# Attention on TensorE by two pairs of heads in one visit, all by quarters of the array

**Chip, cores, metric.** One core of one Trainium2 chip. The metric is the device time of one execution in microseconds (us). Each kernel was executed several times, in turns with the kernel before on the same chip. All times quoted are medians with the lowest and highest in brackets.

## The reference

Attention with RMS-normalised queries and keys (8 batches, 12 heads, 448 positions, head size 64), then a two-layer network with Silu on the 3584 x 768 result. All is float32.

```python
def _attn_ref(q, k, v, g_q, g_k):                     # (8, 12, 448, 64) each
    q_n, k_n = rmsnorm(q, g_q), rmsnorm(k, g_k)       # x / sqrt(mean(x*x) + 1e-6) * g
    scores = np.matmul(q_n, k_n.transpose(0, 1, 3, 2)) / np.sqrt(64)
    attn = np.exp(scores - max)
    attn = attn / (sum of attn + 1e-09)
    return np.matmul(attn, v)
# bridge: (B,H,S,D) -> x (B*S = 3584, H*D = 768)
def _moe_ref(x, w_in, w_out):                         # w_in (768, 2048), w_out (2048, 768)
    h = x @ w_in
    return (h * (1.0 / (1.0 + np.exp(-h)))) @ w_out
```

## The kernel before

The two big products use seven half-size products in place of eight (the class `Seven` and the sums of weights and of `x`). They run on TensorE group by group, a group being two batches. Attention of the next group is dealt in between the products: `fill` runs a share of the products of the group before. Attention goes by pairs of heads, since two heads of 64 fill the 128 rows of the array. Scores take 64 rows and 128 columns at a time, two heads beside each other. Weighted sums take 128 rows and 64 columns. The last 64 keys of two pairs share a 128-row unit and already run by quarters (64 x 64).

```python
def transpose(n, name):                      # n: a pair of heads
    t = ps.tile([P, BANK], F32, name=tr(max(n - 1, 0)))      # one PSUM bank, one tile
    ...
    else:
        for j in range(columns // P):
            nc.tensor.transpose(t[:, ts(j, P)], state[n]["k"][:, ts(j, P)], ident)
        if n < 2 * z.NPAIR:                                   # first group: ScalarE
            nc.scalar.activation(kT[:, 0:columns], t[:, 0:columns], AF.Copy, scale=gains)
        else:                                                 # later: VectorE, once per pair
            nc.vector.tensor_scalar_mul(out=kT[:, 0:columns], in0=t[:, 0:columns], scalar1=gains)

def scores(n, *units):
    for j in units:
        banks = ps.tile([P, 2, BANK], F32, name="sc", bufs=2)
        ...                                                   # two heads: 64 x 128 each
        nc.scalar.activation(e[j][:, h, :], banks[:, h, 0:S], AF.Exp, scale=...)

def weigh(n, *units): ...                                     # 128 x 64, accumulates over keys
def unload(n): nc.scalar.copy(xT(*pairs[n]), state[n]["av"])  # divided later, in SBUF

for n in range(last + 2):                                     # 48 visits, one pair each
    ... scores(n, 0, 1) ... weigh(n - 1, LEFT - 1) ... add_up ... unload(n - 1)
    transpose(n + 1, "q"); weights_in(n, 0); fill(); weights_in(n, 1)
    divide_by_sums(n); scores(n, LEFT - 1) ...
    transpose(n + 1, "k") ... weights_in(n, 2); fill(); weights_in(n, 3); normalise(n + 3)
```

`weights_in` rounds pieces of `w_in`: ScalarE opens one ("L90" in the profiles of the changed kernel below), VectorE takes three steps ("L113" to "L120"), GpSimd one ("L124"). It also forms sums of the rounded weights.

## Time and profile before

| | before |
|---|---|
| time | 1446.68 us (1445.59 to 1447.4, 3 runs) |
| TensorE busy | 97% of 1446.8 us |
| streaming passes, summed over the timeline | 1326 us |
| lost between them | 121 us |
| of which idle before a matmul (over 60 ns) | 34.2 us |
| of which half clock (20.8 us of it, so half is lost) | 10.4 us |
| changes of the array's form (the rows and columns that a matmul takes) | 365 |

All rows but the first two are worked out from the trace. "Streaming" is the sum of full passes at the spacing seen in undisturbed runs of matmuls (0.376 us for 448 columns). "Lost" is the rest of the span. Idle time comes from the matmul records, and half clock from the records of the granted clock.

The view of TensorE's waits says what the 34.2 us were spent on. The columns are the tile and line that waited, the releaser, the total in us, the number of times, and the longest.

```profile
PE mm L624 <- DVE parts L575: 5.6, 7, 1.4
PE end L470 <- DVE work L546: 4.7, 5, 2.3
PE mm L542 <- DVE work L523: 4.7, 2, 3.5
PE end L465 <- ACT x L528: 3.5, 2, 2.2
```

No single wait costs much.

### The profile page before, as it was taken

To read this page: it belongs to the slowest core of one execution; us is meant where nothing else is said; L and a number is where in the kernel's file an instruction comes from. 1 tells how busy PE (TensorE), PEld (TensorE's weight loads), DVE (VectorE), ACT (ScalarE), POOL (GpSimd) and SP (SyncE) were. 2 spreads that over 40 slices of the span, in tenths; PEclk is the share of its full clock that TensorE was granted. 3 is DMA by queue.
4 is the path that set the end of the run, shared out by engine and by line. 5 is a ranking of instruction groups with operands and counts; after the bars stand their busy time and mean duration, and the time that the engine had idled before them with its cause. 6 is when DMAs were issued, how large, how long until landed. Compare 5 with 4: busy or idle time off the path is not lost.

```text
span 1446.8 us, 14152 instructions
## 1 busy us (share of the span) xinstructions
PE 1407.0 (97%) x5033; PEld 682.5 (47%) x5033; DVE 710.1 (49%) x941; ACT 510.5 (35%) x859; POOL 388.2 (27%) x255
## 2 busy tenths in 40 slices
PE   8898999999999999999999999999999999999998
PEld 4333443433444444444444445555555555555554
DVE  5888877766645545654544787721222222222220
ACT  6775456644454455445454354300000000000000
POOL 5564444532323333333421144400000000000000
PEclk9999999999999999999999999999999999999999
DMA  6634245422232232223221267332222222222210
GB/s 184 173 100 115 68 145 146 123 69 72 65 99 73 62 111 62 70 79 94 67 84 42 80 190 227 118 114 74 89 80 82 79 80 81 78 84 80 84 59 25
DMA packets 133269, 137.69 MB, mean 95 GB/s; under 512 B 58052, under 2 KB 113860, under 8 KB 133188
## 3 DMA queue, kind: packets, MB, share of 16 engines
q1 hardware_dynamic: 133120, 136.63, 31.7%
q8 instruction: 42, 0.69, 0.2%
q14 instruction: 39, 0.32, 0.1%
q10 hardware_dynamic: 68, 0.05, 0.0%
HBM read 88.47 MB, written 41.29 MB: 90 GB/s over the span
## 4 chain that ended last, share of the span: by engine, by line
PE 83%; DVE 5%; issue 1%; ACT 1%; DMA 0%; POOL 0%; SPq 0%; DVEq 0%; ACTq 0%; POOLq 0%
PE mm L624 38%; PE end L624 14%; PE sc L624 14%; PE sc L486 7%; PE end L512 7%; DVE work L523 1%; PE end L542 1%; PE end L465 1%; DVE work L546 1%; PE end L470 1%; DVE work L474 0%; DVE W L575 0%; DVE parts L575 0%; DVE stage L575 0%; DVE sums_x L572 0%
## 5 line engine op out<-in xcount | busy, mean ns | idle before, releaser
L624 PE MATMUL mm<-x,W 128*128 128x448 f32 x648 | 261.0, 542 | 4.9 <-DVE parts L575 2.0
L494 ACT ACTIVATE work<-sc,rms 128x448 f32<-128x448 f32 x336 | 187.0, 634 | 148.1 <-PE sc L486 92.7
L365 POOL TENSOR_TENSOR rms<-rms,minus_half 128x14 f32<-128x14 f32 (+3 forms) x49 | 168.3, 3435 | 246.7 <-DVE rms L361 231.5
L624 PE MATMUL mm<-sums_x,W 128*128 128x448 f32 x480 | 196.5, 547 | 5.6 <-DVE parts L575 3.6
L624 PEld LDWEIGHTS mm<-x,W 128*128 128x128 f32 x648 | 118.4, 190 | 111.8 <-issue 96.1
L486 PE MATMUL sc<-work 64*128 64x448 f32 (+1 forms) x768 | 160.9, 582 | 2.1 <-ACT work L472 1.3
L523 DVE TENSOR_TENSOR work<-work 128x896 f32<-128x896 f32 x144 | 160.9, 1118 | 1.7
L512 PE MATMUL end<-work,rows 128*64 128x448 f32 (+1 forms) x768 | 152.2, 561 | 0.0
L644 POOL TENSOR_TENSOR parts<-parts,stage 128x448 f32<-128x448 f32 (+1 forms) x37 | 42.1, 1138 | 341.0 <-DVE parts L575 325.1
L624 PEld LDWEIGHTS mm<-sums_x,W 128*128 128x128 f32 x480 | 87.9, 191 | 87.1 <-issue 70.4
L486 PEld LDWEIGHTS sc<-work 64*128 64x128 f32 (+1 forms) x768 | 53.7, 176 | 102.4 <-issue 84.2
L546 DVE RECIPROCAL work<-end 128x448 f32<-128x448 f32 x25 | 73.9, 2956 | 37.3 <-PE end L542 37.2
L644 POOL TENSOR_TENSOR parts<-parts,W 128x384 f32<-128x384 f32 x9 | 8.9, 992 | 307.6 <-DVE parts L575 307.6
L512 PEld LDWEIGHTS end<-work,rows 128*64 128x64 f32 (+1 forms) x768 | 38.3, 135 | 101.5 <-issue 90.7
L575 DVE TENSOR_TENSOR stage<-mm,parts 128x448 f32<-128x448 f32 (+1 forms) x59 | 36.3, 615 | 87.6 <-PE mm L624 49.4
L755 ACT ACTIVATE stage<-stage 128x896 f32<-128x896 f32 x64 | 58.4, 945 | 41.3 <-DVE stage L575 40.3
L631 ACT COPY stage<-mm 128x448 f32<-128x448 f32 (+1 forms) x34 | 17.9, 526 | 152.5 <-PE mm L624 136.4
L624 PE MATMUL mm<-W,work 128*128 128x384 f32 x204 | 68.6, 486 | 0.0
L624 PE MATMUL sc<-W,work 128*128 128x384 f32 x192 | 64.5, 486 | 0.0
L624 PE MATMUL end<-W,work 128*128 128x384 f32 x192 | 64.5, 486 | 0.0
L474 DVE TENSOR_SCALAR work<-end,gains 128x512 f32<-128x512 f32 (+1 forms) x36 | 24.6, 685 | 63.8 <-PE end L470 63.7
L347 DVE TENSOR_REDUCE rms<-qn 112x8 f32<-112x512 f32 x48 | 32.7, 681 | 41.7 <-ACT qn L346 41.7
(135 smaller groups left out, 1772.5 us busy)
## 6 DMA issues: line engine op xcount, KB each, us to landing
hidden<-stage SPq DMA_DIRECT2D x64, 448.0 KB, 2.8
work<-hidden SPq DMA_DIRECT2D x7, 2048.0 KB, 9.7
x<-hidden SPq DMA_DIRECT2D x7, 2048.0 KB, 9.1
W<-in_moe_w_in_dram SPq DMA_DIRECT2D x24, 512.0 KB, 4.4
rows<-in_moe_w_out_dram SPq DMA_DIRECT2D x32, 384.0 KB, 3.3
rows<-in_q_dram SPq DMA_DIRECT2D x48, 224.0 KB, 3.4
rows<-in_k_dram SPq DMA_DIRECT2D x48, 192.0 KB, 3.8
rows<-in_v_dram SPq DMA_DIRECT2D x48, 192.0 KB, 2.7
```

The lines of the kernel that those rows point to most:

```text
L347: nc.vector.tensor_reduce(out=rms[0 : z.R, 0:nq].rearrange("p (h j) -> p h j", h=2), in_=by_head, axis=AX.X, op=ALU.add,)
L365: nc.gpsimd.tensor_tensor(out=flat, in0=flat, in1=half, op=ALU.pow)
L474: nc.vector.tensor_scalar_mul(out=kT[:, 0:columns], in0=t[:, 0:columns], scalar1=gains)
L486: nc.tensor.matmul(banks[ds(i * size, size), h, 0:S], kT[rows, ds(j * P + i * size, size)], qT[m % 2][rows, :], start=True, stop=True,)
L494: nc.scalar.activation(e[j][:, h, :], banks[:, h, 0:S], AF.Exp, scale=rms[n % 4][:, column : column + 1],)
L512: nc.tensor.matmul(state[m]["av"][ds(h * D, D), :], v, e[j][rows, h, :], start=(j == (LEFT if m % 2 else 0)), stop=(j == (LEFT - 1 if m % ...
L523: nc.vector.tensor_tensor(out=t[rows], in0=e[0] if j == 1 else t[rows], in1=e[j][rows], op=ALU.add)
L546: nc.vector.reciprocal(out=r[0], in_=t)
L575: nc.vector.tensor_tensor(out=out, in0=a, in1=b, op=ALU.add)
L624: nc.tensor.matmul(t, self.left(name, s), self.right(name, s), start=s == ends[0], stop=s == ends[1])
L644: nc.gpsimd.tensor_tensor(out=u2, in0=u2, in1=p5, op=ALU.add)
L755: nc.scalar.activation(t, t, AF.Silu)
```

## The change

The intent is to process two pairs of heads (four heads) in one visit. All attention matmuls then take the same form, 64 x 64 quarters with four at once, and the array changes form only at the ends of a visit. The accumulators are divided straight from PSUM. VectorE's small work is dealt out among the products (`fill(others)`). Row sums of the first group are formed by TensorE in three terms.

```diff
+def transpose_k(c):                           # c: two pairs of heads, 24 visits
+    t = ps.tile([P, 2, BANK], F32, name="sc", bufs=2)        # one tile of two PSUM banks
+    rows = place[f"k{c % 2}"]
+    for i in range(2):                                        # i: which pair, its own bank
+        for j in range(z.KEYS + 1 - i):
+            nc.tensor.transpose(t[:, i, ts(j, P)], rows[:, ds((z.KA, z.KB)[i] + j * P, P)], ident)
+        columns = (z.KEYS + 1 - i) * P
+        nc.vector.tensor_scalar_mul(
+            out=kT[:, ds((z.KA, z.KB)[i], columns)], in0=t[:, i, 0:columns], scalar1=gains
+        )
+def scores(c, j, i=None):
+    ...
+            nc.tensor.matmul(
+                banks[ds(half * D, D), h, 0:S], keys[rows, ts(half, D)], qT[rows, pair, :], ...)
+def weigh(c, j, step=0):
+    if step != weighed["step"]:
+        nc.tensor.drain()                     # before the two pairs swap halves of the rows
+        weighed["step"] = step
+    ...
+def divide(c, source):                        # from PSUM, or in place for the first group
+    for i in range(2):
+        nc.vector.tensor_tensor(out=x, in0=x if source is None else source[i], in1=r[i], op=ALU.mult)
-def fill():
-    while filler["due"] > 0:
-        filler["due"] -= next(filler["work"], filler["due"])
+def fill(others=()):
+    ... # runs the products and calls others[dealt]() evenly among them
-    rounds = {(1, 1), (1, 3), (3, 1), ... }   # pieces of w_in at four points of a visit
+    pieces_at = {0: 1, 1: 1, 2: 1, 3: 1, 4: 2, 5: 1, 6: 2, 7: 3}
+    sums_at = {-1: 1, 1: 0, 5: 2, 8: 3}
+def between(c):
+    transpose_q(c + 1)
+    if 0 < c <= EARLY: divide(c - 1, None)
+    ...
+    late = add(c, LEFT - 1) + add(c, LEFT) if c >= GROUP else []
+    further = normalise(c + 2) if c >= GROUP else []
+    fill(late + weights_in(c, 0) + further[2:])
+    transpose_k(c + 1)
+    sum_up(c)
+    ...
+    fill(weights_in(c, 1) + further[:2])
 (cut: loads, normalisation, the order within a visit, start and end)
```

## The prediction

> **What bounds the kernel now.** I read the page first: busy shares, then the chain that ended last, by engine.
>
> ```profile
> PE 1407.0 (97%) x5033; PEld 682.5 (47%) x5033; DVE 710.1 (49%) x941; ACT 510.5 (35%) x859; POOL 388.2 (27%) x255
> ...
> PE 83%; DVE 5%; issue 1%; ACT 1%; DMA 0%; POOL 0%; SPq 0%; DVEq 0%; ACTq 0%; POOLq 0%
> ```
>
> TensorE is busy 97% of the span and is 83% of the chain; no other engine passes half. So only TensorE time counts, but "busy" includes ends that are modelled, and hides what is lost between matmuls. For that I took the timeline of TensorE, one window from the middle of the long stage:
>
> ```profile
> 508.65 1.77 PE L486 MATMUL sc<-work 64*128 64x448 f32 x8
> 510.35 0.97 PE L512 MATMUL end<-work,rows 128*64 128x448 f32 x4
> 511.26 0.60 PE L465 MATMUL end<-ident,qn 112*128 112x112 f32 x4
> 511.70 3.94 PE L624 MATMUL mm<-sums_x,W 128*128 128x448 f32 x10
> 515.47 1.67 PE L624 MATMUL mm<-x,W 128*128 128x448 f32 x4
> 517.07 0.96 PE L542 MATMUL end<-work,ones 128*32 128x448 f32 x8
> 517.96 1.94 PE L486 MATMUL sc<-work 64*128 64x448 f32 x12
> 519.82 1.72 PE L512 MATMUL end<-work,rows 128*64 128x448 f32 x8
> ```
>
> Read start to start. The ten product records (each f32 matmul leaves two) take 511.70 to 515.47, 3.77 us: **0.376 us a pass** over 448 columns with the whole array. Eight score records are two units of two concurrent heads, four full passes, 1.504 us, but take 1.70: 0.20 lost. Four weighted-sum records are two passes, 0.752, and take 0.91: 0.16 lost. The four product records before L542 lose 1.60 - 1.504 = 0.10 at their end alone. So each change between the forms 64*128, 128*64, 64*64, 128*32 and 128*128 costs about 0.09 on leaving and 0.05 (64 or 32 weight columns) to 0.10 (128 columns) on entering. Transposes and products share a form and lose only about 0.06.
>
> I then summed full passes (0.376; 0.323 for 384 columns; 0.11 and 0.096 a transpose) over the timeline by stage, called "streaming":
> - start, 0 to 11.55: 4.5 streaming, 7.0 lost;
> - A, attention of the first 12 pairs, 11.55 to 134.77: 85.2 streaming, 38.0 lost, of which 13.8 are plain idle gaps;
> - B, attention of 36 pairs among three groups of products, to 815.78: 611.7 streaming, **69.3 lost**, 16.3 of it gaps; 274 changes of form, so (69.3 - 16.3)/274 = 0.19 us each;
> - C, last group of first products, to 935.38: 1.5 lost; D, output products: 5.0 lost.
>
> Together 1326 streaming and 121 lost. The matmul work itself does not shrink, so the change can win only from the 121.
>
> **What the Trainium skill says.** "TensorEngine Tiling (Array Packing)", Key Properties: "Changing tiling mode (not just tile) drains the TensorE". The trace agrees: 0.19 us. Its Gotcha 1 says that different row tiles cannot use one PSUM bank at the same time; that is why the new weighted sums put the two pairs in two banks and drain before they swap halves of the rows. No record of before shows such a drain. "TensorE: Matmul & The Clock Gate", LDWEIGHTS: TensorE pulls weight loads ahead of running matmuls; the 0.376 spacing agrees, and the 0.05 to 0.10 on entering a form is my reading of a load that could not be pulled ahead. "VectorE: DVE Perf Modes", Why PSUM operands drop a tier: f32 with a PSUM operand runs at 1x. L575 (PSUM operand) has 622 ns, L572 (SBUF alone) 621 ns for 128x448: dividing from PSUM costs no more than dividing in place.
>
> **The change part by part.**
> (1) *One form, half as many visits.* A unit (128 keys, 448 queries, two heads) becomes four 64x64 matmuls at once instead of two halves: still two passes, 0.752. The last keys of each two pairs already run so:
>
> ```profile
> L486 PE MATMUL sc<-work 64*64 64x448 f32 x192 | 25.2, 581 | 0.0
> ...
> L512 PE MATMUL end<-work,rows 64*64 64x448 f32 x192 | 23.6, 562 | 0.0
> ```
>
> 192 records are 24 units; 25.2/24 = 1.05 us with a change on either side, so the quarters do stream together. Scores and weighted sums now follow each other without a change. Per two pairs there remain four changes: into quarters (0.145), out to transposes (0.13), to the sums with 32 columns (0.145) and back to products (0.197), 0.62. Stage B has 18 such visits: 11.1 us in place of 53.0. **-41.9.**
> (2) *Drains.* Each visit has two explicit drains, where the weighted sums swap halves. Estimate: the next matmul starts after the end of the last one (modelled at 0.536 after its start) and not 0.376 after it, and its weights load unhidden (0.05) with some 0.07 to restart: 0.28. 36 in stage B: **+10.**
> (3) *Waits within a visit.* A visit has no products in it to cover the exponentials. I walked it by hand: 14 units x 0.752 = 10.5 us on TensorE against 14 x 0.553 = 7.7 on ScalarE (x4 take 2.21 in the timeline), exp starting 1.07 after its scores, two score buffers. All orders fit but one: the weighted sum of the second unit of keys comes some 0.25 before its exp is done. The next visit's first weighted sums need the banks that the division from PSUM frees (2 x 0.62), which fits with nothing to spare. 18 x 0.3 = 5.4. Stalls of products on their two banks (L624 behind DVE and ACT, about 10 of the gaps before) I keep at 8, three group boundaries at 1 each. Gaps 16.4, as before: **0.**
> (4) *Sums.* Before: 20 sums of two pairs (eight records, four at once) and 8 of a single pair (four records, two at once), 40 + 16 = 56 passes. After: two passes in each of 18 visits and six in each of the first 6 (three terms summed by TensorE in place of DVE adds): 72. 16 x 0.376 = **+6.0**, of which stage A takes 36 - 10 = 26 passes, +9.8, and B -3.8.
> (5) *Unloading.* 48 ACT copies (L528, 25.9 us busy), four of six DVE adds per two pairs in A and 4 of 28 reciprocals (2.96 each) go. All lie beside TensorE: nothing by itself, it makes (3) fit.
> (6) *Stage A.* Two pairs take 18.7 us (57.32 to 76.05) without products. After: 14.3 streaming (10.5, transposes 1.54, sums 2.26), changes and drains 1.2, and waits at the turn, where DVE has adds, divisions, weight rounding and the kT copies in line before the next scores: about 1.2. 6 x 2.4, plus 3 for a cold clock and 4 for the second load of q: 21 to 22 lost in place of 38. **-16**, before the +9.8 of (4).
> (7) *Start.* Four powers on GpSimd in line (the two of 8 columns took 3.29 together) before the last q is scaled, and one wider copy: **+2.** *End:* the reserve of partial products goes, but four products still cover the last division and sums: **+1.5.**
>
> Sum: -41.9 + 10 + 0 + 6.0 - 16 + 2 + 1.5 = -38.4. I give back 4.7 of it for waits that I have not seen: 1446.7 - 33.7 = **1413 us**.
>
> **The rivals.** *TensorE waits in the visits.* Everything that hides exp is outside them now. If exp starts 0.3 later, or DVE is still busy with a 2.96 reciprocal when the division is due, each visit loses 1 to 2 us; 24 x 1.5 = 36 eats the gain: about 1447. For it: the only filler stands between the visits, and the page's costliest waits of scores are on ACT. Against it: the walk has slack at all other orders, and ACT is at 35%.
> *Quarters do not stream at full pace.* Twice as many instructions, four weight loads a pass. If a pass took 0.42 in place of 0.376, 672 passes of attention (2 x 168 units x 2) would add 30: about 1442. Against it: the four loads of a 64*64 unit start 6 to 7 ns apart and overlap, and the second pass starts 0.428 after the first just as for 128*64 on entry. But no two such units follow each other in this trace.
> *Drains dear.* At 0.8 each, 48 cost 25 more: about 1438.
> *Better than thought.* If stage A closes up to 3 lost per visit less, or drains cost no more than a change of form: about 1398.
> DMA is at 32% of its engines' span with landings of some 3 us and loads a visit ahead; I do not see it becoming a wait, save for the second q.
>
> **Range and chances.** Part (1) is measured well (+-5). Drains (+-8), waits in visits (+-10), stage A (+-9) and start and end (+-3) are estimates; in squares about 17, and a little less as some of it is shared. What I have not seen mostly costs. Range **1393 to 1434**. The line of 2% is at 1418, 5 above the estimate, so faster by over 2% is 0.58, within 2% 0.38, slower by over 2% 0.04.
>
> **What would show it.** Right: between products the timeline has one long run of 64*64 records per two pairs, with 0.376 between passes; changes of form fall from 365 to about 100; streaming rises by 6 and losses in B fall from 69 to about 38; stage D is unchanged within 1 us; the first scores come near 13.5. Part (2) shows as the spacing at the swap of halves. Wrong, if idle before weighted sums released by exp, or before `av` tiles released by DVE, sums to over 15 us in B; if the quarter passes are spaced by more than 0.39; or if stage A takes over 125 us.

## The result

The changed kernel takes **1528.53 us** (1525.84 to 1532.19, 4 runs) against 1446.13 (1445.43 to 1447.4) of the kernel before beside it. The ratio is 1.057 [1.0543, 1.0597]: 5.7% slower, and far outside the predicted range.

| worked out from the trace, us | before | after |
|---|---|---|
| streaming | 1326 | 1332 |
| lost | 121 | 192 |
| idle before matmuls | 34.2 | 105.7 |
| lost to half clock | 10.4 | 43.1 |
| the remainder (forms, drains, short ends) | 76 | 43 (54 with nothing taken off twice) |
| changes of form | 365 | 97 |

The change did what it was meant to do. The changes of form went, and the remainder fell by 22 us. Idle time rose by 71 us and half clock by 33. (In the changed kernel 22 us of the idle time lie under half clock. The rows take half of that, 11 us, off twice, so the remainder is 54 and not 43. Before, no idle time lay there.)

From the page of the changed kernel, the busy share and the chain that ended last:

```profile
PE 1413.1 (93%) x6281; PEld 712.2 (47%) x6281; DVE 681.0 (45%) x936; ACT 471.4 (31%) x778; POOL 356.1 (23%) x256
...
PE 78%; DVE 12%; ACT 4%; issue 2%; DMA 2%; POOL 1%; SPq 0%; ACTq 0%; DVEq 0%; POOLq 0%
```

VectorE is less busy than before (681 against 710 us), yet its share of the chain rose from 5% to 12%. So the amount of its work does not explain the loss; what stands in its queue at the moment when TensorE asks may. The waits of TensorE name the place:

```profile
PE sc L542 <- DVE work L544: 54.6, 24, 8.1
PE mm L721 <- DVE stage L675: 11.6, 5, 7.3
PE av L594 <- DVE x L643: 7.7, 1, 7.7
PE sc L562 <- ACT work L567: 3.6, 3, 2.0
```

L542 is the transposes of keys and L544 is VectorE's copy of them to `kT`. It happens 24 times, once per visit, and it alone makes up 54.6 of the 105.7 idle us. A visit late in the kernel shows how. First TensorE, then VectorE in the same stretch (columns: start, duration, engine, line, operation, shapes, count, idle before and its releaser):

```profile
405.81 1.67 PE L721 MATMUL mm<-sums_x,W 128*128 128x448 f32 x4
407.32 0.60 PE L542 MATMUL sc<-ident,rows 128*128 128x128 f32 x4
410.69 0.55 PE L542 MATMUL sc<-ident,rows 128*128 128x128 f32 x3 [2.78 <-DVE work L544]
411.17 0.96 PE L626 MATMUL sc<-work,ones 128*32 128x448 f32 x8
```

```profile
408.55 0.61 DVE L675 TENSOR_TENSOR stage<-mm,stage 128x448 f32<-128x448 f32 x1
409.23 0.55 DVE L393 TENSOR_REDUCE rms<-squares 128x6 f32<-128x384 f32 x1
409.81 0.17 DVE L417 TENSOR_SCALAR rms<-rms 128x14 f32<-128x14 f32 x1
409.89 0.74 DVE L544 TENSOR_SCALAR work<-sc,gains 128x512 f32<-128x512 f32 x1
```

The first four transposes are done by 407.92. VectorE is still at the work that was dealt in before them and copies only at 409.89. The three transposes of the second pair then begin at 410.69, after that copy, though they write the other bank of the tile. The Trainium skill, "PSUM — Partial Sum Buffer", PSUM bank collisions, says that accesses of two engines on different banks ran clean. By that page the chip does not ask for this wait. It goes with the order of calls: transposes of pair 0, copy of pair 0, transposes of pair 1, all on one tile. That the dependency is put on the tile and not on the bank is my reading; the trace shows only the wait.

In the stage in which `w_in` is rounded it is worse:

```profile
269.09 0.60 PE L542 MATMUL sc<-ident,rows 128*128 128x128 f32 x4
...
272.84 0.67 ACT L90 ACTIVATE W<-W 128x512 int32<-128x512 uint32 x1 [6.48 <-DMA W<-in_moe_w_in_dram]
...
274.35 0.64 ACT L392 ACTIVATE squares<-rows 128x512 f32<-128x512 f32 x1
275.03 0.69 DVE L393 TENSOR_REDUCE rms<-squares 128x8 f32<-128x512 f32 x1 [4.86 <-ACT squares L392]
...
276.97 0.74 DVE L544 TENSOR_SCALAR work<-sc,gains 128x512 f32<-128x512 f32 x1
...
277.77 0.90 PE L542 MATMUL sc<-ident,rows 128*128 128x128 f32 x3 [8.09 <-DVE work L544]
```

Read it backwards. The transposes wait 8.09 us for the copy. The copy stands in VectorE's queue behind a reduction (L393), which waits for ScalarE's squares (L392). The squares stand in ScalarE's queue behind the opening of a piece of weights (L90), which waits 6.48 us for a load. A load on which the transposes do not depend holds TensorE through the queues of two engines.

The clock follows. The Trainium skill, "TensorE: Matmul & The Clock Gate", HAM oscillation, gives as its rule of thumb that idle gaps of over some 3.4 us throttle the array to half clock. The trace agrees in part. Half clock comes in stretches of 3.41, 6.83 and 10.24 us, and one of 10.24 us begins at 272.5, in the middle of the wait above. There are 14 such stretches before the last few us of the span, against 5 in the kernel before. But shorter gaps bring it too: for six of the 14, no gap that ended in the 7.5 us before the stretch, or that it began in, was over 2.2 us long.

What held is seen in the visit that follows:

```profile
422.92 0.98 PE L562 MATMUL sc<-work 64*64 64x448 f32 x8
423.72 1.68 PE L594 MATMUL av<-work,rows 64*64 64x448 f32 x16
425.22 0.93 PE L562 MATMUL sc<-work 64*64 64x448 f32 x8
426.32 0.98 PE L594 MATMUL av<-work,rows 64*64 64x448 f32 x8 [0.16 <-issue]
427.31 2.03 PE L562 MATMUL sc<-work 64*64 64x448 f32 x16
429.16 0.93 PE L594 MATMUL av<-work,rows 64*64 64x448 f32 x8
429.91 0.93 PE L562 MATMUL sc<-work 64*64 64x448 f32 x8
```

Eight quarters are two passes. 429.16 to 429.91 is 0.75 us, and so is each half of 423.72 to 425.22: quarters stream at full pace. The drain between 425.22 and 426.32 costs 1.10 - 0.75 = 0.35. Two places (426.32 to 427.31, and 427.31 to 429.16) hold 0.24 and 0.35 more.

### The profile page after: what moved, and what is told of

It is laid out like the page before. It is cut to its first block, busy times and chain, and to the rows that moved or that the text cites. A ratio compares the mean times of both kernels' runs of the same rounds, so it can differ in the third digit from the quotient of the medians. Undisturbed runs are those within 1.5% of the kernel's fastest.

```text
span 1524.0 us, 16671 instructions
## 1 busy us (share of the span) xinstructions
PE 1413.1 (93%) x6281; PEld 712.2 (47%) x6281; DVE 681.0 (45%) x936; ACT 471.4 (31%) x778; POOL 356.1 (23%) x256
## 4 chain that ended last, share of the span: by engine, by line
PE 78%; DVE 12%; ACT 4%; issue 2%; DMA 2%; POOL 1%; SPq 0%; ACTq 0%; DVEq 0%; POOLq 0%
PE mm L721 31%; PE sc L721 14%; PE av L721 13%; PE av L594 7%; PE sc L562 7%; DVE work L632 2%; DVE rms L393 2%; DVE work L608 1%; PE sc L626 1%; PE mm L626 1%; PE sc L542 1%; DVE work L544 1%; ACT work L567 1%; ACT squares L392 1%; PE sc L529 1%
## 5 line engine op out<-in xcount | busy, mean ns | idle before, releaser
L421 POOL TENSOR_TENSOR rms<-rms,minus_half 112x16 f32<-112x16 f32 (+4 forms) x50 | 133.2, 2665 | 264.5 <-DVE rms L417 263.5
L562 PE MATMUL sc<-work 64*64 64x448 f32 x1344 | 170.4, 562 | 5.0 <-ACT work L567 3.6
L594 PE MATMUL av<-work,rows 64*64 64x448 f32 x1296 | 155.1, 550 | 16.1 <-DVE x L643 7.7
L608 DVE TENSOR_TENSOR work<-work 128x896 f32<-128x896 f32 (+1 forms) x114 | 121.7, 1101 | 89.7 <-ACT work L567 78.2
L594 PEld LDWEIGHTS av<-work,rows 64*64 64x64 f32 x1296 | 52.2, 134 | 106.5 <-issue 87.3
L393 DVE TENSOR_REDUCE rms<-squares 112x8 f32<-112x512 f32 (+1 forms) x86 | 56.2, 654 | 89.7 <-ACT squares L392 89.3
L562 PEld LDWEIGHTS sc<-work 64*64 64x64 f32 x1344 | 54.0, 136 | 89.3 <-issue 47.1
L542 PE MATMUL sc<-ident,rows 128*128 128x128 f32 x168 | 30.3, 301 | 58.4 <-DVE work L544 54.6
L721 PE MATMUL av<-W,work 128*128 128x384 f32 x192 | 64.5, 486 | 0.0
L124 POOL TENSOR_TENSOR W<-W 128x512 int32<-128x512 int32 x24 | 31.7, 1322 | 137.9 <-DVE W L120 84.3
L392 ACT ACTIVATE squares<-rows 112x512 f32<-112x512 f32 (+2 forms) x79 | 47.6, 603 | 50.3 <-DVE rms L393 47.2
```

Of the source, the lines that this page charges most:

```text
L124: nc.gpsimd.tensor_tensor(out=wi, in0=wi, in1=low, op=ALU.add)
L392: nc.scalar.activation(t, rows, AF.Square)
L393: nc.vector.tensor_reduce(out=out, in_=t.rearrange("p (n d) -> p n d", n=n), axis=AX.X, op=ALU.add)
L421: nc.gpsimd.tensor_tensor(out=t, in0=t, in1=half, op=ALU.pow)
L542: nc.tensor.transpose(t[:, i, ts(j, P)], rows[:, ds((z.KA, z.KB)[i] + j * P, P)], ident)
L562: nc.tensor.matmul(banks[ds(half * D, D), h, 0:S], keys[rows, ts(half, D)], qT[rows, pair, :], start=True, stop=True,)
```

## The experiments

Theory: TensorE waits for VectorE's `kT` copy because of the order of calls within one tile, and VectorE reaches that copy late because of the small work dealt in ahead of it. The kernel before ran beside each set of runs (1445.45 to 1446.97 in the median). Differences are of medians; where two kernels were run in different sets, going through the kernel before changes the difference by up to 1.5 us. Rivals: what the change costs by itself (drains, form, division from PSUM), or simply the amount of VectorE's work.

### The copies of keys after all transposes

```diff
         for i in range(2):
             for j in range(z.KEYS + 1 - i):
                 nc.tensor.transpose(...)
+        for i in range(2):
             columns = (z.KEYS + 1 - i) * P
             nc.vector.tensor_scalar_mul(...)
```

> The changed kernel with one loop split: all seven transposes of the keys are issued before the first of the two copies out of that PSUM tile. Theory: the changed kernel is slow because the second half of the transposes waits for VectorE to copy the first half out of the same tile (54.6 us of TensorE idle over 24 visits, released by the kT copy), and because those gaps let the clock fall. Then the 54.6 go to under 8, granted clock rises from 0.972 to about 0.985, and the time falls by 60 to 75 to 1455 to 1470. Rival (VectorE's queue is what is late, the wait only shows it): the idle moves to products or scores and the time stays over 1510. Rival (the exponentials have no products beside them): the transposes hardly matter, under 15 us.

Measured: 1473.48 us (1472.58 to 1474.35), ratio 1.0182 [1.0165, 1.0199] to before. That is **55 us less** than the changed kernel, by one line, and 5 short of what was expected. The wait is gone from the list of waits, and the seven transposes are one run:

```profile
415.35 1.67 PE L722 MATMUL mm<-x,W 128*128 128x448 f32 x4
416.85 0.93 PE L542 MATMUL sc<-ident,rows 128*128 128x128 f32 x7
417.71 0.96 PE L627 MATMUL sc<-work,ones 128*32 128x448 f32 x8
```

Idle falls from 105.7 to 72.4 and the half-clock loss from 43.1 to 18.6. So 54.6 us of wait gave 33 of idle and 24 of clock. Part of the idle came back elsewhere: products now wait longer for their banks (14.8 and 10.9 in place of 11.6 and 2.9). The list of waits now begins:

```profile
PE mm L722 <- DVE stage L676: 14.8, 5, 8.7
PE mm L722 <- DVE parts L676: 10.9, 8, 4.6
PE av L595 <- DVE x L644: 7.7, 1, 7.7
```

### The pieces of weights spread, with and without that line

```diff
-    pieces_at = {0: 1, 1: 1, 2: 1, 3: 1, 4: 2, 5: 1, 6: 2, 7: 3}
+    pieces_at = {0: 1, 1: 1, 2: 1, 3: 2, 4: 1, 5: 1, 6: 2, 7: 2, 8: 1}
-        fill(late + weights_in(c, 0) + further[2:])
+        w = weights_in(c, 0)
+        fill(w[:1] + late + further[2:] + w[1:])
-        fill(weights_in(c, 1) + further[:2])
+        w = weights_in(c, 1)
+        fill(w[:1] + further[:2] + w[1:])
```

On top of the line above:

> As e1, and the pieces of w_in that are rounded two or three together are set apart: at most two in a fill, one at its start and one at its end. Theory: in stage B ScalarE stands 5 to 7 us in its queue for the second piece's load and VectorE behind it, so products wait (7.3 us at 342) or transposes (8.1 and 6.8). Expected: 8 to 15 us under e1, mostly before 420 us of the trace. Rival (e1 has already hidden it, as the products cover VectorE's delay): within 4 us of e1.

Measured: 1458.64 (1456.29 to 1463.51), ratio 1.0085 [1.0058, 1.0113], a further 15 us less. Idle is 62.5 and the half-clock loss 9.5, close to the 10.4 of the kernel before.

Alone, on the changed kernel:

> The changed kernel with the spread pieces alone, the transposes as they are. Theory (two causes, the long waits of the transposes come from loads in ScalarE's queue, the ordinary ones of 0.8 to 3.5 us from adds and rounding in VectorE's): 15 to 25 us faster than the changed kernel, 1503 to 1513, with transposes still idle for about 40. If the pieces were the whole cause it would fall below 1480.

Measured: 1513.02 (1509.9 to 1513.88), ratio 1.0447 [1.0427, 1.0467], 15.5 us less than the changed kernel. The transposes still wait 45.4 us. The two edits add up (55 and 15 of 70 us). The order of calls makes TensorE wait at all, and the crowd ahead of the copy bears on how long: the longest of these waits fell from 8.1 to 3.6 us.

### What a change of form is worth

Scores of whole units as two 64 x 128 matmuls, as before, on top of the first edit. This puts back nine changes of form per visit, 212 in all (97 become 309).

```diff
+        if j < LEFT:
+            for h in range(2):
+                nc.tensor.matmul(banks[:, h, 0:S], kT[rows, ds(... + j * P, P)], qT[rows, i, :], ...)
-        for half in range(2):
+        for half in range(2 if j == LEFT else 0):
```

> As e1, but the scores of whole units go back to two matmuls of 64 rows by 128 columns; weighted sums stay in quarters. Nine changes of form come back in each of 24 visits. Theory of the prediction (a change of form costs 0.19 us and the visits are bound by TensorE): 35 to 41 us slower than e1. Rival (the visits are bound by the exponentials, so that changes of form hide behind them): under 15 us slower.

Measured: 1495.2 (1490.27 to 1496.87), ratio 1.0319 [1.0295, 1.0344], 21.7 us over its base. That is **0.10 us for each change**, where I had 0.19, and between what the theory (35 to 41) and the rival (under 15) said. Between 375 and 800 us, where neither kernel is at half clock, the loss outside idle time rises from 20.9 to 31.6 us with 102 more changes, which gives the same 0.10. Some of these changes fall beside a drain or a short wait for an exponential, so 0.10 is what they cost here in net. All of them are between 64 x 128 and 64 x 64; changes to and from 128 rows, which are most of those that the change took away, were not priced in this way.

### VectorE's pile at the group's turn

In the seventh visit the first weighted sum waits 7.7 us for the division. In the list of waits this is `av` behind `x`. Ahead of the division stand a reciprocal, rounding, sums of weights and sums of `x`. This edit of the spread kernel moves them ahead: two of the sums of weights half a visit earlier, a double piece of weights into the second visit, and the first sums of `x` behind the division.

```diff
-    sums_at = {-1: 1, 1: 0, 5: 2, 8: 3}
+    sums_at = {-2: (1, (0, 1)), -1: (1, (2, 3)), 1: (0, range(4)), ...}
-        work = [piece] * (1 if c < GROUP else pieces_at.get(i, 0))
+        work = [piece] * ({2: 2, 2 * GROUP - 1: 0}.get(2 * c + half, 1) if c < GROUP else ...)
+        if c == GROUP - 1:
+            sum_x([0, 1], 0)
```

> As e2, and VectorE's work at the turn from the sixth to the seventh visit is set apart: one piece of w_in is rounded in the second visit in place of the sixth, the four sums of w_in's second chunk are split over two fills, and the first sums of x are made as soon as their x is divided. Theory: the 7.7 us that the weighted sums of the seventh visit wait for the division (and some 3 us of half clock after it) come from VectorE's queue at that place alone. Then that gap goes to under 1.5 and the time falls by 8 to 11 from e2, to about 1449. Rival (the division from PSUM waits there whatever VectorE has in line, for the reciprocals' spreading by DMA): under 3 us.

Measured: 1465.14 (1461.49 to 1467.14), ratio 1.0138 [1.0121, 1.0155], 6.5 us **worse** than its base (8.0 through the kernel before). The expectation failed. The wait for the division fell from 7.7 to 4.2, but the moved work now stood ahead of the `kT` copies of the same turn, and scores waited 4.7 us for those. The work had only been moved from in front of one dependent to in front of another.

### Drains, and division from PSUM

Two more drains per visit than that kernel has, 48 in all:

```diff
+        nc.tensor.drain()
         scores(c, 1, 0)
 ...
+        nc.tensor.drain()
         scores(c, LEFT)
```

> As e5, with two more drains of TensorE in each of 24 visits, at places where nothing else waits. It prices the drain. Reading of the trace of e2: 0.32 of delay and 0.04 to 0.05 of an unhidden load, so 48 x 0.36 = 17 us slower than e5. The prediction's 0.28 would give 13, the rival's 0.8 would give 38.

Measured: 1477.29 (1476.97 to 1479.42), ratio 1.0216 [1.0199, 1.0233]. That is 12.2 us over its base, or 0.25 a drain. Between 375 and 800 us the loss rises from 31.0 to 41.1 for some 23 drains, 0.44 each; 2.0 us of that are new waits for exponentials. The change's own 48 drains are thus worth 12 to 21 us. They do not explain the result.

The accumulator copied from PSUM and divided later in SBUF, as in the first group, in all visits but the last:

```diff
-    EARLY = GROUP - 1
+    EARLY = NC - 1
```

> As e5, but x is copied out of PSUM and divided in SBUF afterwards in every visit but the last (it was so in the first five only). It undoes the part of the change that divides from PSUM. Theory (VectorE has room in the steady visits, and a copy frees the bank no later than a division): within 5 us of e5, either way. If dividing from PSUM is what keeps VectorE's queue short, over 8 us slower.

Measured: 1467.96 (1466.75 to 1468.6), ratio 1.0154 [1.0137, 1.0171], 2.8 us over its base. Dividing from PSUM is worth little.

### Smaller orders of work, with a mistake of mine

That kernel with the reciprocal in two halves, Silu one at a time, and another start.

```diff
-        nc.vector.reciprocal(out=r[0], in_=t)
+        nc.vector.reciprocal(out=r[0][:, 0 : S // 2], in_=t[:, 0 : S // 2])   # the rest later, in fill
-                        activate(owed)
+                        activate(owed[:1])
+                        del owed[:1]
```

> As e5, and three waits that its trace should still show are shortened: the reciprocal of 2.96 us in two halves with other work between them, the two Silu of a block at two boundaries of products in place of one, and the keys' second half normalised behind the first transposes at the start. Theory: a product has two banks and so tolerates 2.26 us of delay of its reader; the reciprocal (2.96) and the pair of Silu with its table load (3.07) exceed that once in nearly every visit, 0.6 plus some 0.2 each. Expected 8 to 14 us under e5, so 1435 to 1441, just under the kernel before. If those waits were already hidden: within 3 us of e5.

Measured: 1461.09 (1459.09 to 1461.61), ratio 1.0102 [1.0085, 1.0119], and a **wrong result** (relative error 0.086). I put it down to my change of the start, not to the change studied. I normalised the second half of the first keys after `transpose_k(0)`, which already issues the next load into the same buffer. (The other two edits come back below in a correct kernel.) The time is 4.1 us under its base, where 8 to 14 were expected: the half-clock loss rose from 14.2 to 25.0. It tells one thing all the same, since every stretch after the start does the same work: between 375 and 800 us it loses 23.8 us where its base loses 31.0.

### The turn again, without the pile in front of the copies

On the spread kernel: the accumulator of the sixth visit is copied and divided later, the first sums of `x` move one turn later, two of the four sums of weights move into the seventh visit, and one piece of weights moves from the seventh to the ninth. (The text below says that the sums of `x` go into the turn before, and leaves the piece out; the edit is as said here.)

```diff
-    EARLY = GROUP - 1
+    EARLY = GROUP
-    pieces_at = {0: 1, 1: 1, 2: 1, 3: 2, 4: 1, ...}
+    pieces_at = {1: 1, 2: 1, 3: 2, 4: 2, ...}
-    sums_at = {-1: 1, 1: 0, ...}
+    sums_at = {-1: (1, (0, 1)), 0: (1, (2, 3)), 1: (0, range(4)), ...}
```

> This is e2 with three moves at the turn from the sixth visit to the seventh, where the first weighted sum waited 7.74 us for the division, behind a VectorE queue that held the reciprocal, a piece of rounded weights, four sums of weights and two sums of x: the first sums of x go into the turn before, two of the four sums of weights into the seventh visit, and the sixth visit's accumulator is copied and divided later. Theory (VectorE's order of work at the turn, not its amount, costs the time there): the wait of 7.74 falls under 3, nothing grows before the scores of the visits around it, time 8 to 10 us under e2, about 1449. Rival (moved work comes back as another wait, as it did in e5, whose time was 6.5 over e2): 1456 to 1462.

Measured: 1461.42 (1459.74 to 1462.55), ratio 1.0103 [1.0087, 1.0118]. This is no gain over 1458.64, and the rival won. The wait of 7.7 became one of 3.7, now for the copy of the accumulator. Some other waits grew (products for VectorE 14.1 in place of 12.9, scores for ScalarE 3.1 in place of 1.6), and idle time as a whole fell by only 2.1 us, to 60.4. The half-clock loss rose from 9.5 to 16.3.

On top of it, Silu one at a time from the second group on, and the reciprocal in halves from the seventh visit on, where the sums lie in a tile of the scores and not of the products:

> e9 with two more orders of work, both from e7, whose steady stage lost 23.8 us where e5's lost 31.0: from the second group of products on, ScalarE does one Silu at a time in place of two in a row, and from the seventh visit on VectorE does the reciprocal in two halves with the second half among the spread work. Products in the steady stage then stall less on their banks (about 0.6 us each). Theory: 6 to 9 us under e9, about 1441, so 0 to 0.6 per cent under the kernel before and right in its result. Rival (the stalls come from work that is merely moved): within 2 us of e9.

Measured: 1451.12 (1449.4 to 1453.76), ratio 1.0036 [1.0023, 1.005], correct, **10.3 us less**. Between 375 and 800 us the loss falls from 31.3 to 24.6. Which of the two edits gives how much is not separated.

Is this gain one that the kernel before could have had too? For the Silus, no:

> The kernel before with nothing changed but the order of the Silus from the second group on: one at a time in place of two in a row. It tells whether the gain of e10 over e9 belongs to the change at all. The kernel before loses 5.1 us in idle gaps in 425 us of its steady stage, so there is little to win: expected 0 to 6 us faster than before, 1440 to 1446.

Measured: 1445.99 (1444.35 to 1448.93), ratio 0.9998 [0.9984, 1.0012]. The kernel before is deaf to it. The reciprocal in halves and the orders of the next section were not tried on the kernel before.

### Weights opened at the head of their work

What is left in that version, in its list of waits:

```profile
PE mm L735 <- DVE stage L689: 11.9, 9, 3.3
PE av L595 <- DVE x L1031: 7.5, 6, 3.7
PE mm L735 <- ACT stage L748: 7.0, 2, 6.4
PE sc L563 <- ACT work L568: 5.9, 4, 4.3
```

ScalarE's copy L748 follows 9.41 us of idle that a transfer ended. An opening of weights (L90) idles 6.42 us for a load, with the exponentials behind it, and scores wait 4.3 for those. So a piece is now opened at the head of the work that rounds it, not behind the piece before it. The second step of the normalisation is called after the accumulators' copies.

```diff
+        def opened():
+            if room.w_in.opened == room.w_in.rounded:
+                room.w_in.open()
-        work = [piece] * (1 if c < GROUP else pieces_at.get(i, 0))
+        work = [piece] * (c < GROUP) + [opened, room.w_in.round] * pieces_at.get(i, 0)
 ...
-        run_all(beside[1:2])          # was ahead of the copies or divisions
         if c > 0:
             weigh(c - 1, LEFT - 1, 1)
             ... copies or divisions ...
+        run_all(beside[1:2])
```

> e10 with two orders changed. First, a piece of weights is opened by ScalarE at the head of the work that rounds it, not behind the piece before it, so that ScalarE no longer stands in line for a load issued only just before (in e10 it stands 6.42 us for such a load at 307 us, with a scores wait of 4.28 behind it, and 9.41 us for another transfer at 223 us, with a product wait of 6.36). Second, within a visit the second step of the next normalisation is called after the accumulators' copies, so that VectorE's copies no longer wait behind norm reductions that wait for ScalarE (3.7 us at 142.66 and 3.8 in five visits before). Theory (what is left of the early loss are waits in in-order queues): both waits fall by half or more, 6 to 12 us under e10, 1439 to 1445. Rival (the waits come from amounts of work or from transfers that are late whatever the order): within 3 us of e10, 1448 to 1454.

Measured: **1442.15 us** (1439.06 to 1443.99), ratio 0.9974 [0.996, 0.9989], correct: 9 us less, and 0.26% under the kernel before. The waits at the head of the list are smaller:

```profile
PE mm L735 <- DVE stage L689: 8.8, 5, 3.3
PE mm L735 <- ACT stage L742: 4.2, 1, 4.2
PE sc L563 <- ACT work L568: 4.1, 5, 2.3
```

Of the two orders, the second shows: the waits of `av` for copies fall from 7.5 to 2.1 us. The first does not show as it was meant. ScalarE still idles 19.6 us for the loads of these pieces (17.3 in its base). At 283.46 it stands 9.49 us for one, and a product waits 4.2 behind it, the second line above. Other things stand behind the loads now: the scores that waited 4.3 us at 311 and the product that waited 6.4 at 224 do so no more. What each order gives was not separated.

Idle is 44.0 us in all (before: 34.2). The half-clock loss is 10.4, streaming 1332 and the loss 107 of the span of 1439.0 (before: 121). Of the way from 1528.5 to 1442.2, every step is an order of calls, but for one accumulator that is copied before it is divided and reciprocals that are cut in two; no matmul, drain or form differs.

## Why the prediction was wrong

The sign was wrong: 1413 was predicted and 1528.5 measured, 115 us apart. Point by point:

- **The step that failed is part (3), "Waits within a visit", with its sum "Gaps 16.4, as before: 0".** I walked the visit from its first score to its last and never the turn between two visits. There a single edge costs 54.6 us of idle: 0.9 at the start, 11.5 in stage A and 42.2 in B, where the whole sum had 16.4. Calling the copies last gave back 55 us, in idle time and in clock. Part (6) did name "the kT copies in line before the next scores" in stage A, among 1.2 us per visit. It took them as a delay of scores; that transposes of the second pair wait for the first pair's copy was in none of my steps or rivals.
- **The amount of VectorE's work misled me.** I argued from its 49% share. It does less after the change and holds TensorE longer, since what counts is what stands ahead of the copy that TensorE wants. The spread of the pieces (15 us), the Silus with the reciprocals (10.3) and the order of openings and steps (9.0) show this; the two edits of the turn that failed (6.5 and 2.8 worse) show that a wait is easily only moved.
- **The clock was allowed for only in part (6).** Half clock cost 43.1 us against 10.4 (11 of the 43.1 fell on time that was idle anyway).
- **Stage A** was to lose 21 to 22 us in place of 38. It lost 43.2 in the changed kernel. In the last version its attention (16 to 134 us) loses 21.8. The estimate fits what the stage can do, not what the change did.
- **Part (1), mis-sized.** The count was right (365 to 97, predicted about 100). The price of 0.19 was all that stage B lost outside idle time, divided by its changes, so whatever else was lost there counted as form. Putting 212 changes of one kind back cost 0.10 each, but that price is not shown for the other kinds. The balance of stage B says more: outside idle time and half clock it lost 52 us before and 34 in the last version (134 to 801 us), 18 less, where parts (1) and (2) promised 32. With its 36 drains at 0.25 to 0.44 (9 to 16 us), my estimate for the 202 changes that went there (274 to 72) is 27 to 34 us, 0.13 to 0.17 each, and not 41.9.
- **Part (2), about right.** Predicted 0.28 a drain; 0.35 in the timeline, and 0.25 on average to 0.44 in the steady stretch when added. Rival three (drains dear, 0.8) is out.
- **Rival one** put the waits at the exponentials and divisions within a visit. The 0.24 and 0.35 in the visit shown are about what I had walked for exponentials (the trace names no releaser for them). The division was late once, 7.7 us. As sums go, its 1413 + 36 is 1449 and not 1447. Rival two (quarters not at full pace) is out: 0.376 a pass.
- **Parts (4), (5) and (7).** Streaming 1326 to 1332 as predicted (+6). What unloading gave by itself was not tried alone; dividing from PSUM in place of copying gave 2.8 us. The start took 17.4 us in place of 11.55, where +2 was predicted. The last two stages lose as little as before (0.1 and 4.8).
- **The range.** I combined the errors of the terms that I had listed. A term left out has no error bar: 4% for "slower by over 2%" was a statement about the list, not about the kernel.

Even with its orders mended, the changed kernel is only 0.26% faster: the changes of form were worth less than I took, the drains give part of it back, and the turns keep waits that I did not get rid of. Three things stay open. Some of the mended orders might help the kernel before as well; of these only the Silus were tried there. The last version loses 107 us where the prediction implies 81 (1413 less 1332); 13 of these 26 are idle time between 134 and 375 us (23.8 against 10.7 before), the rest I have not split. And whether the transposes waited on the tile and not the bank was not tried with two tiles; the run with the copies called last shows only that the order of calls removes the wait.

## What to carry to other kernels

When a change moves small work to new places in an in-order queue, list for each engine what stands ahead of every result that the bounding engine waits for, at each turn as well as inside the loop; the shares of busy time say nothing about it. Finish all writes to a PSUM tile before the first read of it is called, or give each half a tile of its own (not tried here). Do not let a queue wait for a load that is needed later than what stands behind it, and look at the granted clock beside every long wait, for it falls with them.

## What the Trainium skill lacked or had wrong

- "TensorEngine Tiling (Array Packing)", Key Properties, says that a change of mode drains TensorE, without a price. Here it cost at most 0.19 us as an average of the losses before, and 0.10 us when 212 changes between 64 x 128 and 64 x 64 were put back.
- No page gives the price of an explicit drain of TensorE: 0.35 us in the timeline of the changed kernel, and 0.25 (whole kernel) to 0.44 us (steady stretch) each for 48 added ones.
- "PSUM — Partial Sum Buffer", PSUM bank collisions, does not warn that a kernel can wait all the same when one tile spans two banks and its halves are written and read in turn: 24 waits, 54.6 us, gone when the copies were called last.
- "TensorE: Matmul & The Clock Gate", HAM oscillation, gives 3.4 us as the gap to stay under. Here shorter gaps did not keep the clock up: six of 14 stretches at half clock came with no gap over 2.2 us near them. The stretches of 3.41, 6.83 and 10.24 us sum to 81.9 us after against 17.1 before, not counting the last few us of each span.
